# One of three DVE shifts per quad moved to GpSimd, in two forms, with the SBUF port that the two share added to the scheduler's model

## The chip, the cores and the metric

The kernel runs on one core of one Trainium2 chip. The metric is the device time of one execution in microseconds. The kernel before takes 803.38 us (median of 3 runs, 802.87 to 804.33). All runs compared here are of the fast state; one of e1's four runs counts as slow and is left out of the comparisons.

## The reference, cut to what matters

Two independent layers on 2048 tokens of width 512 are computed and their outputs concatenated. Layer A is an attention with 32 query heads of width 16 that share one key and one value head; layer B is a linear attention with softmax feature maps. Layer A's exponentials decide: 32 x 2048 x 2048 of them.

```python
q = (x @ wq).reshape(B, S, H, Dh).transpose(0, 2, 1, 3)     # H = 32, Dh = 16
k = x @ wk;  v = x @ wv
scores = einsum("bhqd,bkd->bhqk", q, k) * Dh ** -0.5
p = softmax(scores, axis=-1)
o = einsum("bhqk,bkd->bhqd", p, v)
... # output projection; then layer B, concatenated
```

## The kernel before: the parts that matter

The scores come from PE (TensorE) in tiles of 128 x 512. Two engines share their exponentials. ACT (ScalarE) does it directly, three or two tiles per instruction. DVE (VectorE) uses an approximation in "quads" of four tiles: it writes `Z1 * score + Z0` as int16, whose bits are read as fp16. This is a piecewise linear power of two. Three copies, shifted by 256, 512 and 768 in the integer, are further such functions. PE sums all four with the weights `K[0..3]` in the value matmul. A quad so costs DVE four operations that read PSUM and three "shifts" from SBUF to SBUF, and PE 16 value matmuls in place of 4.

```python
Z1 = 1477.3197218702985
NQ = 3                                   # ring of quad buffers
self.Z = sb("Z", [128, self.NQ, 4, 4, 512], I16)       # [.., plane t, tile h, 512]
...
def bits():                              # "dz": one per tile
    o = Z[:, 0, h, :]
    self.add("dve", lambda v: v.tensor_scalar(out=o, in0=ps[:, bank, :], scalar1=self.Z1, scalar2=self.Z0, op0=ALU.mult, op1=ALU.add), ...)
...
def shift(t):                            # "dS": three per quad
    def go():
        self.add("dve", lambda v: v.tensor_scalar(out=Z[:, t], in0=Z[:, 0], scalar1=256.0 * t, scalar2=None, op0=ALU.add),
                 reads=zk, writes=[("Zt", p, t)])
...
for t in range(1, 4):
    self.job(("dS", quad, t), "dve", 0.60, shift(t), after=[("dz", k - x) for x in range(4)], prio=2)
self.job(("dpv", quad), "pe", 0.87, lambda: self.d_pv(quad), mode="col", prio=1.4, after=[("dS", quad, t) for t in range(1, 4)] + ...)
```

The order of all instructions is made when the program is built. A list scheduler gives every job an engine, a duration (0.60 us for a shift), dependencies and a priority. It always takes the job that can start first, and it decides in the same way which tiles become quads for DVE. Its times are only a model. On the chip each engine runs its own list in order, and only the semaphores for data dependencies hold the engines together. What the plan assumes beyond that is not enforced.

## Time and profile before

| | before |
|---|---|
| time | 803.38 us |
| busy: PE, ACT, DVE, GpSimd (POOL) | 94%, 93%, 91%, 2% |
| tiles on DVE / ACT | 500 (125 quads) / 1548 |
| DVE shifts | 375, 248.6 us busy |

The page's first part gives the busy time of each engine, its share of the span and its instructions:

```profile
span 799.4 us, 17471 instructions
## 1 busy us (share of the span) xinstructions
PE 751.3 (94%) x7462; PEld 246.6 (31%) x7462; DVE 727.6 (91%) x1261; ACT 746.8 (93%) x688; POOL 17.2 (2%) x49
```

The same for two stretches of 300 us (columns as named in the header of the view: PE, weight loads, DVE, ACT, POOL, then the granted PE clock, the DMA share and GB/s):

```profile
60.00:360.00 300.00, 285.06 (x3044) 92.36 (x3043) 298.90 (x518) 293.77 (x277) 4.63 (x9) 1.00 0.12 9
360.00:660.00 300.00, 287.72 (x2774) 96.40 (x2771) 273.69 (x464) 293.02 (x270) 0.72 (x2) 0.99 0.14 15
```

DVE is full in the first stretch (298.9 of 300 us) and ACT is nearly full in both. A shift taken from DVE therefore helps only if the scheduler then gives DVE more tiles, so that ACT has fewer.

The groups, each with line, engine, operation, tiles and shapes, count, busy time, mean ns of one, and the idle time before it:

```profile
L1657 ACT ACTIVATE f_PT<-f_ps 128x1536 bf16<-128x1536 f32 x310 | 456.8, 1474 | 29.4 <-PE f_ps L1602 23.0 <-PE f_ps L1699 5.2
L1749 DVE TENSOR_SCALAR f_Z<-f_ps 128x512 int16<-128x512 f32 x500 | 327.9, 685 | 28.6 <-PE f_ps L1602 28.4
L1762 DVE TENSOR_SCALAR f_Z<-f_Z 128x2048 int16<-128x2048 int16 x375 | 248.6, 689 | 1.0
L1830 DVE TENSOR_TENSOR f_On<-f_accS,f_denS 128x512 bf16<-128x512 f32 x31 | 21.2, 685 | 0.7 <-DMA f_denS<-f_denS 0.7
```

The timeline of DVE (start, duration, operation; "x2" is two in a row):

```profile
150.81 1.32 DVE L1749 TENSOR_SCALAR f_Z<-f_ps 128x512 int16<-128x512 f32 x2
152.03 0.71 DVE L1762 TENSOR_SCALAR f_Z<-f_Z 128x2048 int16<-128x2048 int16 x1
152.62 1.31 DVE L1996 TENSOR_SCALAR f_Wq<-f_ps 128x512 bf16<-128x512 f32 x2
```

Neighbours overlap in the record: the shift that starts at 152.03 us is listed with 0.71 us, and the next operation starts 0.59 us later. A shift therefore occupies DVE for 0.60 us and not for 0.69.

GpSimd's only longer elementwise work in this trace:

```profile
L2081 POOL TENSOR_TENSOR f_KVn<-f_kvS,f_mask 128x128 bf16<-128x128 f32 x8 | 4.4, 552 | 340.2 <-DVE f_kvS L2072 339.6
L1445 POOL COPY f_wk_rep<-f_wk_raw 128x512 bf16<-128x512 bf16 x1 | 0.6, 610 | 0.5 <-DMA f_wk_raw<-in_A_wk_dram 0.5
```

### The profile page before, as it was taken

What the parts mean: (1) busy time and instruction counts of PE and PEld (TensorE: products, weight loads), DVE (VectorE), ACT (ScalarE), POOL (GpSimd) and SP (SyncE); (2) the same over time, 40 slices, a digit from 0 to 9 for tenths busy, and PEclk for the clock granted to TensorE, in tenths of its full rate; (3) what the DMA queues carried; (4) which work ended last, traced back from release to release, by engine and by line L of the source; (5) the groups of instructions that cost most, each with busy time, mean ns of one, the idle gap of its engine ahead of it and who ended that gap; (6) DMA issues with size and microseconds to landing.
All of it is one profiled execution on the core that took longest, in us unless ns stands there. A gap on an engine that the chain in (4) does not pass through costs nothing.

```text
span 799.4 us, 17471 instructions
## 1 busy us (share of the span) xinstructions
PE 751.3 (94%) x7462; PEld 246.6 (31%) x7462; DVE 727.6 (91%) x1261; ACT 746.8 (93%) x688; POOL 17.2 (2%) x49
## 2 busy tenths in 40 slices
PE   8999999999999999999999999999999999989995
PEld 2223222323233233333232333333333333333331
DVE  3799999999999999997989898999899999999953
ACT  4989999999999999999999999999999999999953
POOL 5000000000000000020000000000000000000000
PEclk9799999999999999999999999999999999999998
DMA  6561111110111110011101111111011111001111
GB/s 134 118 122 9 9 8 9 9 8 3 9 8 21 22 8 7 4 9 8 9 6 18 34 7 9 28 9 13 4 8 21 25 25 19 8 12 8 15 21 37
DMA packets 45179, 17.10 MB, mean 21 GB/s; under 512 B 37092, under 2 KB 43236, under 8 KB 45096
## 3 DMA queue, kind: packets, MB, share of 16 engines
q1 hardware_dynamic: 45096, 15.93, 16.1%
q8 instruction: 60, 0.98, 0.5%
q14 instruction: 23, 0.19, 0.1%
HBM read 2.15 MB, written 4.19 MB: 8 GB/s over the span
## 4 chain that ended last, share of the span: by engine, by line
DVE 66%; PE 25%; ACT 5%; DMA 1%; issue 1%; SPq 1%; DVEq 0%; POOL 0%; POOLq 0%
DVE f_Z L1749 27%; DVE f_Z L1762 21%; PE f_ps L1602 7%; ACT f_PT L1657 4%; PE f_ps L1787 4%; PE f_ps L1699 4%; PE f_ps L2096 3%; DVE f_vS L2045 2%; PE f_ps L1408 2%; DVE f_ssum L2019 2%; DVE f_accS L1414 2%; PE f_ps L1843 2%; DVE f_On L1830 2%; DVE f_Wk L2156 2%; DVE f_QA L1414 1%; DVE f_mq L1558 1%
## 5 line engine op out<-in xcount | busy, mean ns | idle before, releaser
L1657 ACT ACTIVATE f_PT<-f_ps 128x1536 bf16<-128x1536 f32 x619 | 719.5, 1262 | 38.7 <-PE f_ps L1602 29.9
L1749 DVE TENSOR_SCALAR f_Z<-f_ps 128x512 int16<-128x512 f32 x500 | 327.9, 685 | 28.6 <-PE f_ps L1602 28.4
L1602 PE MATMUL f_ps<-f_QA,f_KR 32*128 32x512 bf16 x2048 | 313.3, 388 | 24.7 <-DVE f_Z L1749 13.4
L1762 DVE TENSOR_SCALAR f_Z<-f_Z 128x2048 int16<-128x2048 int16 x375 | 248.6, 689 | 1.0
L1602 PEld LDWEIGHTS f_ps<-f_QA,f_KR 32*128 32x128 bf16 x2048 | 80.4, 91 | 255.2 <-ACT f_PT L1657 88.2
L1699 PE MATMUL f_ps<-f_PT,f_VA 128*32 128x512 bf16 x1548 | 152.0, 393 | 0.9 <-DVE f_accS L1414 0.5
L1787 PE MATMUL f_ps<-f_Z,f_VK 128*32 128x512 f16 x2000 | 132.3, 385 | 4.0 <-DVE f_accS L1414 1.8
L1408 PE MATMUL f_ps<-f_ones,f_zero 128*128 128x512 bf16 (+9 forms) x234 | 67.7, 357 | 2.0 <-POOL f_zero L1427 1.3
L1699 PEld LDWEIGHTS f_ps<-f_PT,f_VA 128*32 128x32 bf16 x1548 | 38.0, 93 | 92.7 <-issue 82.2
L1787 PEld LDWEIGHTS f_ps<-f_Z,f_VK 128*32 128x32 bf16 x2000 | 42.8, 96 | 63.2 <-DVE f_Z L1762 13.9
L2096 PE MATMUL f_ps<-f_BxT,f_Wq 128*128 128x512 bf16 x128 | 33.2, 382 | 1.6 <-DVE f_Z L1749 1.0
L1408 PEld LDWEIGHTS f_ps<-f_ones,f_zero 128*128 128x128 bf16 (+2 forms) x234 | 18.3, 97 | 34.3 <-issue 22.5
L1843 PE MATMUL f_ps<-f_wo_pad,f_On 128*128 128x512 bf16 x96 | 24.9, 382 | 0.6 <-DVE f_Z L1749 0.6
L2156 DVE TENSOR_TENSOR f_Wk<-f_ps,f_wq 128x512 bf16<-128x512 f32 x32 | 21.9, 685 | 1.7 <-PE f_ps L2145 1.7
L1830 DVE TENSOR_TENSOR f_On<-f_accS,f_denS 128x512 bf16<-128x512 f32 x31 | 21.2, 685 | 0.7 <-DMA f_denS<-f_denS 0.7
L2103 ACT ACTIVATE f_ET<-f_ps 128x512 bf16<-128x512 f32 x32 | 20.8, 649 | 0.6 <-PE f_ps L2096 0.5
L1414 DVE COPY f_accS<-f_ps 128x512 f32<-128x512 f32 x31 | 21.3, 687 | 0.0
L2045 DVE TENSOR_TENSOR f_vS<-f_ps,f_rs 128x1024 bf16<-128x1024 f32 x16 | 19.6, 1225 | 0.0
L2019 DVE TENSOR_REDUCE f_ssum<-f_Ek 128x64 f32<-128x1024 bf16 x16 | 19.5, 1217 | 0.0
L1554 DVE TENSOR_SCALAR f_KR<-f_ps,f_half 128x512 bf16<-128x512 f32 x8 | 5.6, 745 | 15.1 <-PE f_ps L1546 15.1
L1592 PE MATMUL f_ps<-f_AxT,f_wq 128*128 128x512 bf16 x64 | 18.0, 408 | 0.0
L2013 ACT ACTIVATE f_Ek<-f_ps 128x512 bf16<-128x512 f32 x32 | 17.8, 625 | 0.1
(95 smaller groups left out, 323.3 us busy)
## 6 DMA issues: line engine op xcount, KB each, us to landing
f_denS<-f_denS SPq DMA_DIRECT2D x124, 30.0 KB, 3.0
out_dram<-f_outB SPq DMA_DIRECT2D x18, 128.0 KB, 1.8
f_denC<-f_accS SPq DMA_DIRECT2D x124, 2.0 KB, 1.7
f_denS<-f_denC SPq DMA_DIRECT2D x124, 2.0 KB, 1.7
out_dram<-f_outA SPq DMA_DIRECT2D x14, 128.0 KB, 1.7
f_wq<-in_A_wq_dram SPq DMA_DIRECT2D x1, 512.0 KB, 4.2
f_Bwv<-in_B_wqkv_dram SPq DMA_DIRECT2D x1, 512.0 KB, 5.1
f_Bwo<-in_B_wo_dram SPq DMA_DIRECT2D x1, 512.0 KB, 8.3
```

The source lines that it names most:

```text
L1408: mm = pe.matmul(ps[0:m, bank, 0:n].rearrange("p (a n) -> p a n", n=128), lhsT=zero[0:r, 0:m], rhs=rhs, start=start, stop=start, **kw)
L1414: self.add("dve", lambda v: v.tensor_copy(out=out, in_=in_), reads=reads, writes=writes)
L1602: return pe.matmul(self.ps[:, bank, :], lhsT=self.KR[32 * g:32 * g + 32, sc % 2, kap * 128:(kap + 1) * 128], rhs=self.QA[32 * g:32 * g + 3 ...
L1657: self.add("act", lambda a: a.activation(out=PT[:, sl[0]:sl[0] + size, :], in_=ps[:, b0:b0 + size, :], func=ACT.Exp), reads=[("PS", b0 + i ...
L1699: mm = pe.matmul(ps[32 * g:32 * g + 32, bank, :], lhsT=w, rhs=PT[:, slots[g], :], start=start, stop=stop, tile_position=(0, 32 * g))
L1749: self.add("dve", lambda v: v.tensor_scalar(out=o, in0=ps[:, bank, :], scalar1=self.Z1, scalar2=self.Z0, op0=ALU.mult, op1=ALU.add), reads ...
L1762: self.add("dve", lambda v: v.tensor_scalar(out=Z[:, t], in0=Z[:, 0], scalar1=256.0 * t, scalar2=None, op0=ALU.add), reads=zk, writes=[("Z ...
L1787: mm = pe.matmul(ps[32 * g:32 * g + 32, bank, :], lhsT=w[:, k, :], rhs=Zf[:, k, sl[g], :], start=start and k == 0, stop=stop and k == 3, t ...
L1830: self.add("dve", lambda v: v.tensor_tensor(out=On[:, sc % 12, :], in0=accS[:, r, :], in1=R[:, r, :], op=ALU.mult), reads=[("accS", r), (" ...
L1843: mm = pe.matmul(ps[:, bank, :], lhsT=On[:, (8 * qc + a) % 12, q0:q0 + 128], rhs=self.wo_pad[:, a, :], start=(a == 0), stop=(a == 7))
L2096: mm = pe.matmul(ps[:, bank, :], lhsT=w[:, dc].rearrange("p x h a f -> p (x h a f)")[:, G * 128:G * 128 + 128], rhs=xT[:, dc, m * 512:(m + ...
L2156: self.add("dve", lambda v: v.tensor_tensor(out=o, in0=i, in1=w.unsqueeze(3).to_broadcast([128, 2, 16, 16]), op=ALU.mult), reads=[("PS", b ...
```

## The change

GpSimd is nearly idle and DVE is full, so the third shift of each quad goes to GpSimd. In even quads it stays the same instruction, an int16 `tensor_scalar`. In odd quads it is one int32 `tensor_tensor` on packed pairs: two int16 values are one int32, the constant holds 768 twice, and no carry crosses. The scheduler is told 2.0 us for both (`PSHIFT`). It is also told that GpSimd and certain DVE jobs (`LOCK`) can't run at the same time. The diff, cut to its core:

```diff
+        self.step3 = sb("step3", [128, 2], I16)            # filled with 768 at the start
 ...
         t = j.rel
+        if j.eng == "pool" or j.name[0] in self.LOCK:
+            t = max(t, self.te_port)
 ...
         self.te[j.eng] = max(self.te[j.eng], start + dur)
+        if j.eng == "pool" or j.name[0] in self.LOCK:
+            self.te_port = start + dur
 ...
-                self.dbusy += 1.2 if h == 3 else -0.6
+                self.dbusy += 0.6 * (self.DSHIFT - 1) if h == 3 else -0.6
 ...
         def shift(t):
             def go():
-                self.add("dve", lambda v: v.tensor_scalar(out=Z[:, t], in0=Z[:, 0], scalar1=256.0 * t, scalar2=None, op0=ALU.add),
+                if t == 3 and quad % 2:
+                    n = Z[:, 0].rearrange("p h n -> p (h n)").bitcast(I32).shape[1]
+                    self.add("pool", lambda v: v.tensor_tensor(out=Z[:, 3].rearrange("p h n -> p (h n)").bitcast(I32), in0=Z[:, 0].rearrange("p h n -> p (h n)").bitcast(I32),
+                                                               in1=self.step3.bitcast(I32).to_broadcast([128, n]), op=ALU.add),
+                             reads=zk + ["step3"], writes=[("Zt", p, t)])
+                    return
+                self.add(eng(t), lambda v: v.tensor_scalar(out=Z[:, t], in0=Z[:, 0], scalar1=256.0 * t, scalar2=None, op0=ALU.add),
                          reads=zk, writes=[("Zt", p, t)])
 ...
+        def eng(t):
+            return "dve" if t <= self.DSHIFT else "pool"
         for t in range(1, 4):
-            self.job(("dS", quad, t), "dve", 0.60, shift(t), ...)
+            self.job(("dS", quad, t), eng(t), 0.60 if eng(t) == "dve" else self.PSHIFT, shift(t), ...)
 ...
+    DSHIFT = 2
+    PSHIFT = 2.0
+    LOCK = ("dS", "on", "aq", "aK")
```

More of the change, by code (lines that the diff above doesn't have):

```diff
@@ L1254, in __init__ @@
         self.tr, self.tw = {}, {}
-        self.fin = 0.0
+        self.fin = self.te_port = 0.0
         self.te_sp = 52.0
@@ L1449, in head @@
             add("pool", (lambda k: (lambda g: g.memset(self.onesK[:, k, :], self.K[k])))(k), writes=["onesK"])
+        add("pool", lambda g: g.memset(self.step3, 768), writes=["step3"])
         add("pool", lambda g: g.memset(self.denS, 1.0), writes=[("denS", 0), ("denS", 1)])
@@ L1492, in head @@
             S.batch_end()
-        for k, t in (("wk_rep", 3.5), ("half1", 3.0), ("wv", 8.2), ("wq", 8.2), ("VA1", 5.0), ("ones", 1.0), ("zero", 1.0), ("bmx", 14.0)):
+        for k, t in (("wk_rep", 3.5), ("half1", 3.0), ("wv", 8.2), ("wq", 8.2), ("VA1", 5.0), ("ones", 1.0), ("zero", 1.0), ("bmx", 14.0), ("step3", 8.0)):
             self.tw[k] = (t, "sp")
@@ L1761, in go @@
             def go():
-                self.add("dve", lambda v: v.tensor_scalar(out=Z[:, t], in0=Z[:, 0], scalar1=256.0 * t, scalar2=None, op0=ALU.add),
+                if t == 3 and quad % 2:
[5 more added lines that the diff above has]
+                self.add(eng(t), lambda v: v.tensor_scalar(out=Z[:, t], in0=Z[:, 0], scalar1=256.0 * t, scalar2=None, op0=ALU.add),
                          reads=zk, writes=[("Zt", p, t)])
-                if self.rec is None:
+                if self.rec is None and eng(t) == "dve":
                     self.dbusy -= 0.6
             return go
+        def eng(t):
+            return "dve" if t <= self.DSHIFT else "pool"
         for t in range(1, 4):
-            self.job(("dS", quad, t), "dve", 0.60, shift(t), after=[("dz", k - x) for x in range(4)], prio=2)
+            self.job(("dS", quad, t), eng(t), 0.60 if eng(t) == "dve" else self.PSHIFT, shift(t), after=[("dz", k - x) for x in range(4)], prio=2)
         self.job(("dpv", quad), "pe", 0.87, lambda: self.d_pv(quad), mode="col", prio=1.4,
```

## The prediction

> **What bounds the kernel now.** The busy-time page has PE 94%, ACT 93%, DVE 91%. By stages, from 60 to 360 us DVE is busy 98.8 to 100% and ACT about 98%; from 360 to 660 us DVE falls to 85 to 94% and ACT stays at 96 to 99%. So two engines share the exponentials and both are full; a shift helps only if the program's own list scheduler turns the freed DVE time into fewer ACT tiles. By the table of groups DVE does 500 score tiles (125 quads of 4), ACT 1548. The timeline shows that consecutive 512-wide DVE operations and shifts start 0.60 us apart although each is listed with 685 to 689 ns, so a quad occupies DVE 7 x 0.60 = 4.2 us. ACT needs about 0.42 us a tile (1474 ns for three), 1.7 us for four.
>
> **Removed.** One of three shifts a quad: 125 x 0.60 = 75 us of DVE. **Moved.** If the scheduler rebalances, n quads obey 3.6n - 525 = -1.7(n - 125) as change of DVE and ACT time: n = 139, and both engines end 24 us earlier (3%). This is the ceiling; PE gets 14 more quads of 16 instead of 4 value matmuls (1.05 against 0.40 us in the timeline), about 9 us, in part taken from its filler matmuls (53 us between 60 and 780 us). I expect 15 to 22 us of it in the plan.
>
> **Added.** About 139 GpSimd instructions. In the trace GpSimd copied 128x512 bf16 in 610 ns and wrote memsets at 0.83 ns per element, so an estimate for the even quads' 2048 int16 elements is 1.8 to 2.3 us. For the odd quads' 1024 int32 pairs the trace's tensor_tensor (552 ns at 128 elements, 322 at 64, strided) would give 3.8 us; the Trainium skill (GPSIMD Engine Reference, Performance versus the Vector engine) gives 4497 ns for 2048 fp32, which halves to about 2.25 us. I take 2.1 and 2.5 us; the plan says 2.0 for both.
>
> **The port.** The skill (SBUF — State Buffer, Who interferes with whom) says that GpSimd and a DVE operation in a two-port mode lock each other out for a whole instruction. The remaining two shifts (2048 int16 in 0.60 us, several elements a cycle) must be such operations. No run here shows it yet. The plan models the lock, but no semaphore enforces its order: a GpSimd start 0.1 to 0.3 us later than planned, or an addition longer than 2.0 us, blocks the next shift, and a full DVE passes that on to PE and ACT. About 0.1 to 0.3 us a quad is 14 to 40 us. Small DVE operations outside the model (the cast into vS, the maximum of bmx, 16 each) can be blocked too, up to 2 us each, some 5 to 15 us. That eats most of the gain.
>
> **Prediction.** 803 - 19 (plan) + 15 (blocked DVE) = 799 us; range 780 to 835. Faster by over 2%: 0.22; within 2%: 0.55; slower by over 2%: 0.23.
>
> **What would show it.** GpSimd busy 280 to 350 us, two groups of about 2.1 and 2.5 us; 132 to 142 quads, ACT tiles down by 30 to 70; the mean of the DVE shifts up from 689 to 750-950 ns, or idle time before them released by GpSimd; DVE busy no lower than before although it does less; operations reading PSUM unchanged at 685 ns; clock about 0.98.
>
> **What would make it wrong.** Integer addition of 3.5 us or more: blocked over 1 us in every odd quad, time above 840 us. No lock in practice, or GpSimd shorter than 2 us with the plan's order kept: 780 us or less. Value matmuls waiting for GpSimd, with three quad buffers too few, would show as PE waiting on GpSimd.

## The result, and the profile after

| | before | after |
|---|---|---|
| time, median (range) | 803.86 us (802.87 to 806.56, 4 runs) | 1094.7 us (1093.94 to 1095.86, 4 runs) |
| ratio of fast runs | | 1.361, 95% interval 1.358 to 1.365 |
| tiles on DVE / ACT | 500 / 1548 | 492 / 1556 |
| granted PE clock | 0.984 | 0.833 |

A ratio is the mean time of one kernel's fast runs over that of the other's fast runs of the same rounds, so it is not quite the ratio of the medians quoted beside it. The result is right; it is only 36% slower.

```profile
span 1093.0 us, 17630 instructions
## 1 busy us (share of the span) xinstructions
PE 868.5 (79%) x7448; PEld 258.1 (24%) x7448; DVE 904.2 (83%) x1124; ACT 763.2 (70%) x692; POOL 489.8 (45%) x173
```

The two stretches, with the columns of before:

```profile
60.00:360.00 300.00, 234.70 (x2156) 69.13 (x2159) 270.08 (x332) 208.11 (x192) 139.83 (x37) 0.84 0.08 7
360.00:660.00 300.00, 236.98 (x2074) 71.66 (x2075) 246.68 (x301) 218.20 (x204) 131.84 (x44) 0.86 0.09 8
```

In the first stretch DVE is still listed as busy for 270 us but completes 332 instructions in place of 518. ACT falls from 294 to 208 us. The groups show what DVE is "busy" with:

```profile
L1663 ACT ACTIVATE f_PT<-f_ps 128x1536 bf16<-128x1536 f32 x311 | 455.0, 1463 | 168.7 <-PE f_ps L1608 166.4 <-PE f_ps L1413 1.2
L1774 DVE TENSOR_SCALAR f_Z<-f_Z 128x2048 int16<-128x2048 int16 x246 | 389.9, 1608 | 0.5
L1774 POOL TENSOR_SCALAR f_Z<-f_Z 128x2048 int16<-128x2048 int16 x62 | 348.6, 5622 | 290.4 <-DVE f_Z L1755 290.2 <-POOL f_Z L1770 0.2
L1755 DVE TENSOR_SCALAR f_Z<-f_ps 128x512 int16<-128x512 f32 x492 | 321.4, 681 | 101.4 <-PE f_ps L1608 99.6
L1770 POOL TENSOR_TENSOR f_Z<-f_Z,f_step 128x1024 int32<-128x1024 int32 x61 | 125.0, 2050 | 290.2 <-DVE f_Z L1755 288.2
L1845 DVE TENSOR_TENSOR f_On<-f_accS,f_denS 128x512 bf16<-128x512 f32 x31 | 33.4, 1079 | 0.8 <-DMA f_denS<-f_denS 0.8
```

Three readings:

- The DVE shift went from a mean of 689 to 1608 ns. There are fewer of them, yet their busy time rose from 248.6 to 389.9 us. Operations that read PSUM did not change (685 to 681 ns).
- GpSimd's int16 form takes 5.6 us and the int32 form 2.05 us. The plan has 2.0 us for both.
- DVE does not have more tiles than before, but 8 fewer. The scheduler made no use of the DVE time that the change freed.

The timeline shows one case (DVE and GpSimd):

```profile
210.56 0.68 DVE L1755 TENSOR_SCALAR f_Z<-f_ps 128x512 int16<-128x512 f32 x1
211.16 6.45 DVE L1774 TENSOR_SCALAR f_Z<-f_Z 128x2048 int16<-128x2048 int16 x2
211.33 5.74 POOL L1774 TENSOR_SCALAR f_Z<-f_Z 128x2048 int16<-128x2048 int16 x1 [10.35 <-DVE f_Z L1755]
217.54 1.21 DVE L2060 TENSOR_TENSOR f_vS<-f_ps,f_rs 128x1024 bf16<-128x1024 f32 x1
```

Two shifts that took 1.3 us together before take 6.45 us. GpSimd was released 0.17 us after the first began. It ends at 217.07 us and the pair at 217.61 us, 0.54 us later, which is about the length of one shift. The second shift had to wait until GpSimd was done. PE then waits for DVE, and ACT for PE. No data dependency runs from this GpSimd operation to these shifts.

### The profile page after: what moved, and what is told of

It reads as the page before. It is cut to its first block, busy times and chain, and to the rows that moved or that the text cites. A ratio compares the mean times of both kernels' runs of the same rounds, so it can differ in the third digit from the quotient of the medians.

```text
span 1093.0 us, 17630 instructions
## 1 busy us (share of the span) xinstructions
PE 868.5 (79%) x7448; PEld 258.1 (24%) x7448; DVE 904.2 (83%) x1124; ACT 763.2 (70%) x692; POOL 489.8 (45%) x173
## 4 chain that ended last, share of the span: by engine, by line
DVE 55%; PE 39%; ACT 2%; issue 1%; DMA 1%; SPq 1%; DVEq 0%; POOL 0%; POOLq 0%
DVE f_Z L1774 29%; DVE f_Z L1755 14%; PE f_ps L1608 13%; PE f_ps L1802 10%; PE f_ps L1705 5%; PE f_ps L1413 2%; ACT f_PT L1663 2%; DVE f_On L1845 2%; PE f_ps L2111 2%; DVE f_vS L2060 1%; DVE f_accS L1419 1%; PE f_ps L1858 1%; PE f_ps L1598 1%; DVE f_ssum L2034 1%; DVE f_Wk L2171 1%
## 5 line engine op out<-in xcount | busy, mean ns | idle before, releaser
L1663 ACT ACTIVATE f_PT<-f_ps 128x1536 bf16<-128x1536 f32 x623 | 731.9, 1248 | 279.7 <-PE f_ps L1608 276.3
L1774 POOL TENSOR_SCALAR f_Z<-f_Z 128x2048 int16<-128x2048 int16 x62 | 348.6, 5622 | 290.4 <-DVE f_Z L1755 290.2
L1608 PE MATMUL f_ps<-f_QA,f_KR 32*128 32x512 bf16 x2048 | 345.0, 442 | 85.9 <-DVE f_Z L1755 48.6
L1774 DVE TENSOR_SCALAR f_Z<-f_Z 128x2048 int16<-128x2048 int16 x246 | 389.9, 1608 | 0.5
L1770 POOL TENSOR_TENSOR f_Z<-f_Z,f_step 128x1024 int32<-128x1024 int32 x61 | 125.0, 2050 | 290.2 <-DVE f_Z L1755 288.2
L1802 PE MATMUL f_ps<-f_Z,f_VK 128*32 128x512 f16 x1968 | 163.0, 462 | 65.9 <-DVE f_Z L1774 59.2
L1705 PE MATMUL f_ps<-f_PT,f_VA 128*32 128x512 bf16 x1556 | 172.2, 441 | 7.3 <-DVE f_accS L1419 6.5
L1413 PE MATMUL f_ps<-f_ones,f_zero 128*128 128x512 bf16 (+9 forms) x244 | 79.8, 405 | 2.1 <-POOL f_zero L1432 1.3
L1845 DVE TENSOR_TENSOR f_On<-f_accS,f_denS 128x512 bf16<-128x512 f32 x31 | 33.4, 1079 | 0.8 <-DMA f_denS<-f_denS 0.8
L2020 PE MATMUL f_ps<-f_Wk,f_BxT 128*128 128x512 bf16 x64 | 20.7, 458 | 8.2 <-DVE f_Z L1755 5.9
```

What stands on the lines that cost most here:

```text
L1413: mm = pe.matmul(ps[0:m, bank, 0:n].rearrange("p (a n) -> p a n", n=128), lhsT=zero[0:r, 0:m], rhs=rhs, start=start, stop=start, **kw)
L1608: return pe.matmul(self.ps[:, bank, :], lhsT=self.KR[32 * g:32 * g + 32, sc % 2, kap * 128:(kap + 1) * 128], rhs=self.QA[32 * g:32 * g + 3 ...
L1663: self.add("act", lambda a: a.activation(out=PT[:, sl[0]:sl[0] + size, :], in_=ps[:, b0:b0 + size, :], func=ACT.Exp), reads=[("PS", b0 + i ...
L1705: mm = pe.matmul(ps[32 * g:32 * g + 32, bank, :], lhsT=w, rhs=PT[:, slots[g], :], start=start, stop=stop, tile_position=(0, 32 * g))
L1770: self.add("pool", lambda v: v.tensor_tensor(out=Z[:, 3].rearrange("p h n -> p (h n)").bitcast(I32), in0=Z[:, 0].rearrange("p h n -> p (h ...
L1774: self.add(eng(t), lambda v: v.tensor_scalar(out=Z[:, t], in0=Z[:, 0], scalar1=256.0 * t, scalar2=None, op0=ALU.add), reads=zk, writes=[(" ...
```

## The experiments

Twelve kernels ran, on three chips (e1 to e4, e5 to e8, e9 to e12), each beside runs of the kernel before on the same chip (medians 802.24, 803.7 and 804.13 us). A difference between runs of different chips is therefore good to about 2 us at best. "Same order" means that the list of jobs on every engine, as the scheduler issues it, is that of the kernel after; this was compared job by job.

My theory after the result was A: the long int16 form holds the shared port, and the DVE shifts wait for it. The rivals were B (any use of GpSimd here, or the new order itself), C (PE waits for a third plane that comes late) and D (GpSimd disturbs every DVE access to SBUF, whatever the port mode).

### e1: the int32 addition in every quad

```diff
-                if t == 3 and quad % 2:
+                if t == 3:
```

> Every quad's third shift is the int32 addition; order of instructions on all engines is that of after. Theory A (the int16 form, 5.6 us against the 2.05 us of the int32 form, holds the port and blocks the DVE shifts): DVE shifts fall from a mean of 1608 ns to 750 to 900, time falls from 1095 to 800 to 840 us. Rival B (any GpSimd use beside DVE, or the order of the plan, is the cost): above 950 us. Rival C (PE waits for the late third plane): as A, so e4 has to tell A from C.

Measured: 871.48 us (863.86 to 878.76; the slowest of the 4 runs counts as slow), ratio 1.084 (1.074 to 1.094). The median of the three fast runs, 867.3 us, is used in what follows; they spread over 12 us.

```profile
L1770 POOL TENSOR_TENSOR f_Z<-f_Z,f_step 128x1024 int32<-128x1024 int32 x123 | 259.2, 2107 | 567.5 <-DVE f_Z L1755 567.4
L1774 DVE TENSOR_SCALAR f_Z<-f_Z 128x2048 int16<-128x2048 int16 x246 | 223.7, 932 | 0.5
```

The form of the instruction alone is worth 227 us (1094.7 - 867.3). That is A's direction, but both numbers missed A's ranges: the shifts are still at 932 ns and the kernel is 8% slower than before, although GpSimd now takes about what the plan assumed.

### e2: the int16 form in every quad

```diff
-                if t == 3 and quad % 2:
+                if False:
```

> Every quad's third shift is the int16 addition of a scalar; order as in after. A: as much slower than after as after is slower than e1, so about 1340 to 1400 us, DVE shifts at a mean of about 2.4 us. B: about 1095 us as after.

Measured: 1238.45 us (1237.12 to 1239.77), ratio 1.543; DVE shifts at a mean of 2031 ns, GpSimd at 5557 ns:

```profile
L1774 POOL TENSOR_SCALAR f_Z<-f_Z 128x2048 int16<-128x2048 int16 x123 | 683.6, 5557 | 512.8 <-DVE f_Z L1755 508.9 <-POOL f_Z L1774 3.7 <-DVE f_accS L1419 0.2
L1774 DVE TENSOR_SCALAR f_Z<-f_Z 128x2048 int16<-128x2048 int16 x246 | 494.1, 2031 | 0.5
```

B expected about 1095 us, so its first half (any use of GpSimd costs the same) is out; its other half, the order, is tested in e3. The time is below the 1340 to 1400 us that I expected from A: the second half of the quads cost less (144 us) than the first half (227 us), so the cost isn't simply proportional, as I had assumed.

### e3: the same order with a GpSimd operation of one pair

The result is wrong. The operation touches one int32 per partition, and the fourth value matmul reads plane 2. (Its output, like that of e4, e7 and e10, still passed the comparison with the reference; the tolerance doesn't see which of two neighbouring planes is read. These runs say something about time only.)

```diff
+                if t == 3:
+                    self.add("pool", lambda v: v.tensor_tensor(out=Z[:, 3, 0, 0:2].bitcast(I32), in0=Z[:, 0, 0, 0:2].bitcast(I32), in1=self.step3.bitcast(I32), op=ALU.add), ...)
+                    return
 ...
-                         mm = pe.matmul(..., rhs=Zf[:, k, sl[g], :], ...)
+                         mm = pe.matmul(..., rhs=Zf[:, min(k, 2), sl[g], :], ...)
```

> Wrong result on purpose: the GpSimd operation touches one pair per partition, and the fourth value matmul reads plane 2. Same order, same waits. A and C: 795 to 815 us, DVE shifts back at 689 ns, clock near 0.98: the order itself is as good as before's. B, if the order is bad by itself: above 850 us.

Measured: 803.77 us (799.71 to 808.3), ratio 1.004 (0.998 to 1.009). The page and one group:

```profile
PE 739.7 (93%) x7379; PEld 248.1 (31%) x7448; DVE 653.2 (82%) x1124; ACT 746.2 (94%) x692; POOL 65.8 (8%) x173
L1778 DVE TENSOR_SCALAR f_Z<-f_Z 128x2048 int16<-128x2048 int16 x246 | 162.4, 684 | 0.5
```

Two things follow. The order itself costs nothing, and with GpSimd out of the way the shifts are at 684 ns and the clock is back at 0.982. But the order also gains nothing: DVE has 74 us less to do than before (653.2 against 727.6) and ACT about as much (746.2 against 746.8), so the time stays. The lower clock in the kernel after (0.833) thus belongs to the stalls and not to the new order; it is low also in e10 (0.754), where PE waits for a slow DVE without any blocking.

### e4: GpSimd as after, but nobody waits for its result

The result is wrong. The `hide` argument takes the third plane out of PE's semaphore dependencies and leaves it in the scheduler's keys, so the order stays.

```diff
-                         mm = pe.matmul(..., rhs=Zf[:, k, sl[g], :], ...)
+                         mm = pe.matmul(..., rhs=Zf[:, min(k, 2), sl[g], :], ...)
-            self.add("pe", fn, reads=sorted(set(rd), key=str), **kw)
+            self.add("pe", fn, reads=sorted(set(rd), key=str), hide=[("Zt", p, 3)], **kw)
```

> Wrong result on purpose: GpSimd does exactly what it does in after (both forms, both lengths, same start), but PE reads plane 2 and waits for no GpSimd operation. A: DVE shifts stay at 1500 to 1700 ns and time at 1040 to 1095 us. C: time falls to 800 to 830 us.

Measured: 1094.49 us (1090.89 to 1096.11), ratio 1.363; DVE shifts at 1612 ns:

```profile
L1774 DVE TENSOR_SCALAR f_Z<-f_Z 128x2048 int16<-128x2048 int16 x246 | 390.9, 1612 | 0.5
```

That is the time of the kernel after to within its own spread. C is out: what GpSimd delivers late costs nothing, and what it occupies costs everything.

### e5: e1, with GpSimd held to the planned order

e1 was not explained by the length of the operation. In its trace I matched each DVE shift that was listed over 0.2 us too long with a GpSimd operation: 44 groups of consecutive shifts, each with one held shift, which ends 0.55 to 0.56 us after GpSimd's end. (The 51 in the text below came from reading the timeline in windows of 12 us; groups cut by a window's edge were counted twice.) In 24 of them GpSimd had been released between 0.04 and 0.17 us after the first shift of the group began. These 24 make 40.8 of the 61.3 us by which e1's shifts are longer than e3's. GpSimd waits only for the data (the last `dz`), so it comes in between two shifts that the plan has back to back. In e5 GpSimd also waits for the last DVE operation that the plan put before it on the port. As the plan has this order anyway, the wait can't deadlock.

```diff
+        if j.eng == "dve" and j.name[0] in self.LOCK:
+            self.lock_task = self.S.prog["dve"][-1]
 ...
-                             reads=zk + ["step3"], writes=[("Zt", p, t)])
+                             reads=zk + ["step3"], writes=[("Zt", p, t)], deps=[self.lock_task])
```

> e1 (int32 addition in every quad, same order on every engine) with one thing added: each GpSimd addition waits for the last DVE operation that the plan put before it on the shared port, so GpSimd can't slip in front of a shift that the plan has first. Theory A1 (in e1 half of the blocked shifts come from GpSimd starting 0.16 us after a pair of shifts, between the two): blocked groups fall from 51 to under 25, DVE shifts from a mean of 932 to 690 to 800 ns, time from 871 to 803 to 835 us. Rival A2 (blocking comes from the length of the addition and drift alone): shifts stay at 880 to 950 ns and time at 860 to 880 us. Rival A3: the waits delay GpSimd so that later shifts are blocked instead, 850 us or more.

Measured: 814.28 us (812.98 to 816.6), ratio 1.014 (1.011 to 1.018). The same count now gives 22 blocked groups, and none in which GpSimd is released after the first shift. The 20 other groups of e1 made 20.5 us, and these 22 make 21.4 us: the wait removed the blocking by early GpSimd operations and left the rest. The groups:

```profile
L1773 POOL TENSOR_TENSOR f_Z<-f_Z,f_step 128x1024 int32<-128x1024 int32 x123 | 232.7, 1892 | 542.0 <-DVE f_Z L1777 282.4 <-DVE f_Z L1758 251.0 <-DVE f_On L1848 8.5
L1777 DVE TENSOR_SCALAR f_Z<-f_Z 128x2048 int16<-128x2048 int16 x246 | 184.8, 774 | 0.5
```

The same two shifts in the timelines of DVE and GpSimd, first in e1:

```profile
416.04 2.98 DVE L1774 TENSOR_SCALAR f_Z<-f_Z 128x2048 int16<-128x2048 int16 x2
416.21 2.27 POOL L1770 TENSOR_TENSOR f_Z<-f_Z,f_step 128x1024 int32<-128x1024 int32 x1 [2.33 <-DVE f_Z L1755]
```

and then in e5:

```profile
393.25 1.28 DVE L1777 TENSOR_SCALAR f_Z<-f_Z 128x2048 int16<-128x2048 int16 x2
394.62 1.89 POOL L1773 TENSOR_TENSOR f_Z<-f_Z,f_step 128x1024 int32<-128x1024 int32 x1 [3.52 <-DVE f_Z L1777]
```

In e1 GpSimd's 2.27 us contain about 0.4 us of its own waiting for the first shift; it then gets the port before the second. In e5 it comes after both, and takes its 1.89 us. The waits brought 53 us (867.3 to 814.3) at an unchanged order. A2 and A3 are out.

### e6: e5, with the small port users in the plan

The job `rs` holds the maximum `bmx`, and `vs` the cast into `vS`.

```diff
-    LOCK = ("dS", "on", "aq", "aK")
+    LOCK = ("dS", "on", "aq", "aK", "rs", "vs")
```

> e5 with the small DVE operations with two inputs from SBUF or a one-input cast (bmx, vS) put into the plan's list of port users; its order differs. A1: 795 to 825 us, bmx back to about 220 ns from 506. It would be the best honest version of the change; I expect no gain over before of more than 1%.

Measured: 796.87 us (791.46 to 800.19, 6 runs), ratio 0.992 (0.988 to 0.996). It computes the right result and beats the kernel before by 0.8%, no more than expected. The maximum `bmx` is at 267 ns, against 504 in e5 (I had expected about 220); the cast into `vS` is at 305, against 497. DVE has 500 tiles, as before.

### e7: no third shift at all

The result is wrong: the job is gone, nobody waits for it, and the fourth matmul reads plane 2.

```diff
-        for t in range(1, 4):
+        for t in range(1, 3):
             self.job(("dS", quad, t), ...)
 ...
```

> Wrong result on purpose: the third shift is done by no engine and waited for by none (the fourth value matmul reads plane 2), and the scheduler knows it. It bounds what any offload of that shift can give. My prediction's balance says 779 us (24 us less). Rival (the freed DVE time isn't turned into fewer ACT tiles, as e3 showed: DVE busy fell by 74 us and the time stayed): 788 to 800 us, ACT busy over 93%, quads at most 130.

Measured: 790.78 us (787.0 to 794.1, 6 runs), ratio 0.985 (0.981 to 0.988).

```profile
PE 732.8 (93%) x7398; PEld 244.1 (31%) x7470; DVE 670.6 (85%) x1154; ACT 739.9 (94%) x684; POOL 15.8 (2%) x50
L1755 DVE TENSOR_SCALAR f_Z<-f_ps 128x512 int16<-128x512 f32 x512 | 333.8, 681 | 53.1 <-PE f_ps L1608 52.3
```

This is all that this scheduler gets out of removing the shift: about 13 us (803.7 to 790.8, or 1.5%). It makes 128 quads (512 tiles), 3 more than before, and not 139. DVE is idle for 15% of the span and ACT stays at 94%.

### e8: the true durations in the plan

```diff
-            self.job(("dS", quad, t), eng(t), 0.60 if eng(t) == "dve" else self.PSHIFT, ...)
+            self.job(("dS", quad, t), eng(t), 0.60 if eng(t) == "dve" else (2.0 if quad % 2 else 5.7), ...)
```

> after with its two forms, but the scheduler is told 5.7 us for the int16 form and 2.0 us for the int32 form. If the wrong duration in the plan is what made after slow, it falls to 820 to 900 us; if the int16 form costs by itself whatever the plan, it stays above 1000 us.

Measured: 983.11 us (978.7 to 987.52), ratio 1.224. This is between the two expectations. The plan with right durations is 112 us faster, but a plan that isn't enforced is still not what runs. It also has 115 quads in place of 123, so that fewer GpSimd operations can block; no run separates this part.

### e9 and e10: DVE shifts that need no second port

In both, the two remaining shifts also write out their accumulator. What the text for e9 takes from the skill stands in the Trainium skill (SBUF — State Buffer, Who interferes with whom). e9 has GpSimd's operations of the kernel after, and e10 those of e3 (wrong).

```diff
+                kw = dict(op1=ALU.add, accum_out=self.junk[:, t:t + 1]) if t < 3 else {}
-                self.add(eng(t), lambda v: v.tensor_scalar(out=Z[:, t], in0=Z[:, 0], scalar1=256.0 * t, scalar2=None, op0=ALU.add), ...)
+                self.add(eng(t), lambda v: v.tensor_scalar(out=Z[:, t], in0=Z[:, 0], scalar1=256.0 * t, scalar2=None, op0=ALU.add, **kw), ...)
```

> after, with GpSimd's two forms, but the DVE shifts also write out their accumulator, which the skill lists as outside the two-port modes. The sums are used by nobody; the result stays right. Alone the shift should then take about four times as long (estimate from the 512-element operations at 0.60 us apart: 2.2 us), so the whole is slower than before by 300 us or more. Theory A (the block is the shared port): the longest shift is within 0.3 us of the shortest although GpSimd overlaps, and time is that of e10 within 2%. Rival D (GpSimd slows or blocks any DVE access to SBUF): shifts of 5 us or more remain and e9 is over 100 us slower than e10.

> Wrong result on purpose: e9 with GpSimd's operation cut to one pair per partition, as in e3. A: same time as e9 within 2%. D: over 100 us faster than e9.

Measured: e9 1227.35 us (1226.22 to 1228.07), e10 1216.12 us (1212.62 to 1219.05): 0.9% apart. Operations with two inputs in SBUF are still held in e9: the sixteen `bmx` and the 31 `On` take 12.3 us longer than in e10 (10.7 and 26.2 against 3.4 and 21.2 us), about the 11 us between the two. The view of the line in e9 (count, then min/median/max in ns):

```profile
L1777 DVE TENSOR_SCALAR_CACHE_REDUCE f_Z<-f_Z x246: 2221/2277/2305, 33.7 to 1205.1; 128x2048 int16<-128x2048 int16 x123
L1777 POOL TENSOR_SCALAR f_Z<-f_Z x62: 5365/5366/5735, 31.2 to 1202.9; 128x2048 int16<-128x2048 int16 x62
```

and in e10:

```profile
L1781 DVE TENSOR_SCALAR_CACHE_REDUCE f_Z<-f_Z x246: 2227/2277/2312, 35.0 to 1197.1; 128x2048 int16<-128x2048 int16 x123
```

This form of the shift takes 2.28 us, always, whether GpSimd works for 5.4 us at a time or hardly at all. Compare it with the kernel after, where single shifts reach 5.85 us. So D is out: the block hangs on the fast form of the DVE shift, which fits the shared port. GpSimd's int16 form takes 5.37 us here at the median, so 5.4 us is its own length. The form is slower for the kernel, of course, as it makes DVE the limit.

### e11: e6 without its waits

e6's `LOCK`, without e5's edit.

> e6 without its waits: same order on every engine. If the waits do the work, as from e1 to e5 (57 us), it is 840 to 870 us; if the longer list of port users in the plan does it, it is 797 to 815 us.

Measured: 850.54 us (849.26 to 852.59), ratio 1.058. The waits are worth 54 us here (850.5 to 796.9), and 53 us from e1 to e5 (the 57 in the text above has e1's slow run in it). The longer list, with the order that the scheduler makes of it, is worth about 17 us with or without them (814.3 to 796.9, and 867.3 to 850.5).

### e12: e8 with the waits

e8, with e5's edit for both forms.

> e8 with the waits of e5: each GpSimd operation waits for the last DVE operation that the plan put before it on the port. If e8's 180 us over before came from GpSimd starting out of the planned order, it falls to 820 to 860 us; if the 5.6 us of the int16 form cost that whatever the order, it stays above 930 us.

Measured: 849.21 us (841.42 to 850.74), ratio 1.054 (1.047 to 1.060). With right durations and an enforced order the two-form kernel loses 5%, not 36%. Its GpSimd operations are at their own lengths, by the view of the line (min/median/max in ns):

```profile
L1777 POOL TENSOR_SCALAR f_Z<-f_Z x58: 5362/5363/5833, 32.8 to 826.4; 128x2048 int16<-128x2048 int16 x58
```

## Why the prediction was wrong, point by point

A table of the runs with the same order on every engine; "blocked" is the busy time of the 246 shifts over the 162.4 us that they take in e3; e1 is given by its fast runs:

| kernel | time, us | shifts busy, us | blocked, us |
|---|---|---|---|
| e3, one pair on GpSimd | 803.8 | 162.4 | 0 |
| e5, int32, order enforced | 814.3 | 184.8 | 22.4 |
| e1, int32 | 867.3 | 223.7 | 61.3 |
| after, both forms | 1094.7 | 389.9 | 227.5 |
| e2, int16 | 1238.5 | 494.1 | 331.7 |

The time follows the blocked shifts, and at the long end rises by more than they do (291 us for 227 from e3 to after): the stalls pass on to PE and ACT, whose waits the profile after lists.

1. **What bounds the kernel: right.** DVE and ACT are both full, and a shift helps only through the balance of tiles. e3 showed it: 74 us less DVE work, no change in time.
2. **"I expect 15 to 22 us of it in the plan", with 132 to 142 quads: wrong.** The kernel after has 123 quads and its order, without blocking, is worth nothing (e3, 1.004). Even without any third shift there are 128 quads and 13 us (e7). My balance assumed that the scheduler fills DVE whenever DVE has time. What holds it at 128 quads was not tested; the rules by which it admits a quad are a candidate.
3. **"I take 2.1 and 2.5 us": the term that failed most.** For the int32 addition 2.5 us was too much (1.89 us unobstructed); the 2.25 us beside it was an estimate, half of the page's figure. For the int16 form I scaled a bf16 copy and memsets, and got 1.8 to 2.3 us for an operation that takes 5.37 us. Other operations and types on the same engine were no measure of this one. (The two forms differ in instruction, type and element count at once; which of these makes the int16 form slow, no run separates.) I named the danger of an addition of 3.5 us or more, with a time above 840 us, but put it on the wrong form.
4. **"About 0.1 to 0.3 us a quad is 14 to 40 us" of blocking: right mechanism, wrong size.** It was 227.5 us over 123 quads, 1.85 us a quad. Two causes multiply. One is the length. The other is that nothing enforced the order: even with 1.89 us on GpSimd the blocking was 0.50 us a quad (e1), and it fell to 0.18 with the order enforced (e5). I had written that no semaphore enforces the order, and had thought of GpSimd being late. It came early: between two shifts that the plan had back to back. In the kernel after this happened 22 times, 16 of them with the int16 form at about 5.2 us each, and it makes 93 of the 227.5 us. The other 50 held shifts, 135 us, met a GpSimd operation that was released at another time.
5. **"Small DVE operations outside the model", 5 to 15 us: right.** From e3 to the kernel after the sixteen `bmx` rose from 3.5 to 10.6 us and the sixteen casts from 4.9 to 6.1, about 8 us together. (The 17 us from e5 to e6 are no measure of this: e6 also has another order and 8 more DVE tiles.)
6. **"Value matmuls waiting for GpSimd": named as a danger and rightly left out of the sum** (e4).
7. **The skill on the port.** The Trainium skill (SBUF — State Buffer, Who interferes with whom) was borne out where it matters. Held shifts in the fast form end 0.54 to 0.56 us after GpSimd does, in the kernel after, e1 and e5 alike. The form with the accumulator, which the page lists as outside the two-port modes, is never held (e9, e10).

How the 291 us divide depends on the order of the steps, as length and order multiply. Changing the form first gives 227 us, the order then 53 us, and 10 us over e3 are left. Telling the plan the true durations first gives 112 us, and the order then 134 us.

## What to carry to other kernels

Before moving an operation to GpSimd, measure that very instruction, with its type: here two ways to add the same constant to the same bytes took 5.37 and 1.89 us. If a static plan relies on the order in which two engines take a shared resource, enforce this order with a semaphore; a model of the resource alone doesn't bind the chip (53 us here). And time freed on a full engine is worth only what the scheduler turns into less work for the other full engine, so run the kernel with the work simply left out, as e7 does, before building the offload.

## What the Trainium skill lacked or had wrong

- GPSIMD Engine Reference, Engine selection, calls one-input elementwise work "roughly line-rate". The int16 `tensor_scalar` on 128x2048 takes 5.37 us, 2.6 ns per element, and the two-input int32 addition on the same bytes takes 1.89 us, 1.85 ns per int32 element. The page has no figure for int16.
- GPSIMD Engine Reference, Performance versus the Vector engine, gives 4497 ns for a two-input addition of 2048 fp32, so 2.25 us for 1024 as an estimate. The int32 addition of 1024, with the second input broadcast, took 1.89 us.
- SBUF — State Buffer, Who interferes with whom, says that whoever issues first gets the pair. It does not say who is next when DVE has a second such instruction right behind the first. In e1 GpSimd was released 24 times during the first of two back-to-back shifts, and got it before the second in all 24.
- SBUF — State Buffer, Summary: rules for kernel authors, says that also a DVE operation with two SBUF inputs fully blocks until a GpSimd operation that reads SBUF finishes. Here it depends on GpSimd's form. Beside the int32 form, each held `bmx` (3 in the kernel after, 4 in e1) ended 0.08 us after GpSimd's end. Beside the int16 form it ended 1.65 us before it: in the kernel after one took 0.97 us and ended at 415.16 us, with GpSimd running from 411.44 to 416.81 us, and the five in e2 show the same 1.65 us. The held `On` operations of the kernel after agree (two end 0.55 us after the int32 form's end, six 1.18 to 1.19 us before the int16 form's). So they are held to a fixed point of the int16 operation that lies before its end; that this is where its reading is over was not shown.
